# Layer slots reordered around one first-layer product: softmax moved, a PSUM bank changed, unread products added

## The chip, the cores and the metric

The kernel runs on one core of one Trainium2 chip, as one launch. The metric is the device time of that launch in microseconds. The core has a matmul engine (PE, with its weight loads PEld), a vector engine (DVE), a scalar engine (ACT), GpSimd (POOL) and a queue engine (SP) that issues DMAs; each works through its own queue in order.

## The reference

Three stages in a row, all float32:

```python
# 1 attention in chunks: 8 batches, 8 heads, 576 tokens in 9 chunks of 64, head size 64
scores = q_c @ k_c.T / 8
attn = exp(scores - max); attn /= sum + 1e-9
x = attn @ v_c                       # then laid out as 4608 tokens x 512
# 2 first layer, 512 -> 1024 -> 512
h = x @ w_in
solu = h * softmax(h)
ln = (solu - mean) / sqrt(var + 1e-6) * g_ln
y = ln @ w_out
# 3 second layer, 512 -> 1536 -> 512
out = (silu(y @ w_gate) * (y @ w_val)) @ w_out2
```

The weights come as float64 and are converted in the kernel.

## The kernel before

The 4608 tokens are 36 tiles of 128; three tiles make a group of 384 tokens (12 groups). Phase one (ph1) does attention and the first layer tile by tile and writes y to DRAM; phase two does the second layer for pairs of groups (lines 714 to 903) and is not touched by the change. Products that need float32 accuracy are split into a high and a low part in a reduced float32 format and done in three passes (`PASSES`, line 148).

The order on every engine is written out by hand: from `tc.manual_schedule()` (line 505) on, an instruction stands in its engine's queue where the program issues it. A buffer of a pool is handed to the next tile of the same tag when all readers of the old tile are done; an engine whose next instruction needs such a buffer stops until then, with all that is behind it.

What one tile t goes through:

- `load_qk`, `load_v`: 256 KB each on SP's queue.
- `scores(t)`: 32 small matmuls into one half of the PSUM tile `so_ps` (s_ps). `softmax(t)`: maximum and difference on DVE, exponential on ACT. `softmax_b(t)`: sum and reciprocal on DVE, the multiplication on POOL (line 299).
- `p_transpose(t)`: four PE transposes into the PSUM tile `pt` (line 307), then ACT copies it to `p` (line 309). `pv(t)`: 32 small matmuls of p and v into the other half of `so_ps` (o_ps). `x_split(t)`: ACT writes the high part of x, DVE (`x_low`) the low part.
- `hidden(t)`: the first layer's product of this tile, 24 matmuls of 512 columns (two halves of 12) into the PSUM tile `h`, of which there is one (two banks).
- `ln_max` (DVE), `ln_exp` (ACT), `ln_b` (DVE; its product with h, line 368, is the last reader of `h`), `ln_c` (a square on ACT, then seven instructions on POOL that end in line 392).
- `ln_T(t)`: eight PE transposes of the normalised tile into the PSUM tiles t0 and t1, the high part by ACT (line 411); the function that it returns, `ln_low`, makes the low part on DVE (line 416).
- `y_run`: the w_out products of a whole group, 24 matmuls of 384 columns for each 128 columns of y, in a PSUM pool of two banks with tag y (`ps_y`); at each 24th an ACT copy to SBUF (line 169) and a DMA to DRAM. `y_upto(t)` says how many are issued up to slot t: none before slot 4, 24 in each of slots 4 and 5, 48 in slot 6, then 32 a slot; the last 96, of group 11, belong to phase two's start (lines 892 to 894).

A slot works on several tiles at once. In the plain slot (lines 601 to 657, t from 4 on) PE's order is: scores(t+2), hidden(t), ln_T(t-1), pv(t+1), w_out products, and at the end p_transpose(t+2). In the same slots a weight of w_out or of the second layer is loaded (`w_raw`, two slots ahead), converted (`conv_start` a slot ahead on ACT and POOL, `conv_b` on DVE, `conv_c` on POOL) and split or spilled to DRAM (`todo2`, one slot later). PSUM is full: `so_ps` two banks, `h` two, t0, t1, and two for tag y. `pt` shares the tag y with the w_out products:

```python
pt = ps_y.tile([P, H, CH], F32, tag="y", name="pt")      # line 305
tr = ps_t.tile([P, 4, P], F32, tag=f"t{half}", name="tr") # line 405
ys[u] = ps.tile([P, TOK], F32, tag=ptags[...], name="y") # line 162
```

Slots 0 to 3 are `first_slot` (lines 659 to 692): no w_out products; softmax(t+1) is done at the head of slot t, behind it hidden(t), p_transpose(t+1), ln_T(t-1), pv(t+1) and scores(t+2). Slot 4 (`Y_AT`) is a plain slot with softmax(5), hidden(4) and p_transpose(5) put at its head (lines 607 to 611), so that it does two softmaxes. The prologue (lines 506 to 582) converts w_in into `wA` piece by piece, and does tile 0's and 1's attention and hidden(0) in its gaps. The end of phase one (lines 707 to 712) is the rest of `todo2`, then the last 32 w_out products but for group 11, then ln_T(35); phase two begins with SP's loads of y (`y_load`), the 96 products of group 11 and the preparation of y's operands (`y_prep`, lines 766 to 771).

Of the kernel before, what the change touches and what calls it, by code (L numbers as in the profile page):

```python
# [8 lines left out]
F32 = mybir.dt.float32  # L9
# [8 lines left out]
P = 128  # L18
CH = 64
GT = 3  # L20
W_OUT = 6
Y_AT = 4
# [4 lines left out]
def attn_moe_moe2_kernel(  # L27
# [16 lines left out]
    H = 8  # L44
# [193 lines left out]
    with ExitStack() as ph1:  # L238
# [63 lines left out]

        def p_transpose(t):
            e = st.pop(t).rearrange("p (n c) j -> p n (c j)", c=2)
            pt = ps_y.tile([P, H, CH], F32, tag="y", name="pt")
            for n in range(NP):
                nc.tensor.transpose(pt[:, 2 * n:2 * n + 2].rearrange("p h i -> p (h i)"), e[:, n], ident)  # L307
            p = att.tile([P, H, CH], F32, tag="p", name="p")
            nc.scalar.activation(out=p, in_=pt, func=AF.Copy)
            st["p", t] = p  # L310

        def pv(t):
            vv, p = vt.pop(t), st.pop(("p", t))
            for i in quads:
                quad(o_ps, vv, p, *i)

        def x_split(t):
            o = o_ps.rearrange("p c n i -> p n c i")
# [175 lines left out]
        def high(*ks):  # L494
            for k in ks:
                nc.scalar.activation(out=wA[:, k, 0, :], in_=cc[k], func=AF.Copy)
# [61 lines left out]
        clp(POOL, 6)  # L558
        add(5)
        hidden(0, (0,))  # L560
        softmax_b(1)
        shf(6)
        rnd(6)
# [12 lines left out]
        add(7)  # L576
        pv(1)
        x_low = x_split(1)
        high(7)
        rest(DVE, 7)  # L580
        hidden(0, (1,))
# [19 lines left out]
        def slot(t, todo2):  # L601


            todo, ahead = w_todo(t), t + 2 < NT
            cs = conv.pop(t)
            outs = [w2_out(u) if k == "2" else None for k, u in todo]
            if t == Y_AT:
                softmax(t + 1)
                softmax_b(t + 1)
                hidden(t)  # L610
                p_transpose(t + 1)
            if ahead:
                scores(t + 2)
                if t + 4 < NT:
                    load_qk(t + 4)
                softmax(t + 2)
            cs[:1] = [conv_c(c, o) for c, o in zip(conv_b(cs[:1]), outs)]
            if ahead:
                softmax_b(t + 2)
            for k, steps in todo2:  # L620
                if k == "o":
                    steps[1]()
            todo2 = [x for x in todo2 if x[0] != "o"]
            if t > Y_AT:
                hidden(t)
            ln_max(t)
            ln_exp(t)
            for k, steps in todo2:
                steps[0]()
            ln_low = ln_T(t - 1) if t >= 1 else None  # L630
            ln_b(t)
            x_low = None
            if t + 1 < NT:
                pv(t + 1)
                if t + 3 < NT:
                    load_v(t + 3)
                x_low = x_split(t + 1)
            if ln_low:
                ln_low()
            if x_low:  # L640
                x_low()
            ln_c(t)
            y0, y1 = y_upto(t - 1), y_upto(t)
            y2 = min(y1, -(-y0 // NY) * NY)
            y_run(wB, y0, y2, ps_y, att)
            for k, steps in todo2:
                steps[1]()
            if t + 1 < NT:
                conv_start(t + 1)
            cs[1:] = [conv_c(c, o) for c, o in zip(conv_b(cs[1:]), outs[1:])]  # L650
            y_run(wB, y2, y1, ps_y, att)
            for k, steps in todo2:
                steps[2]()
            if t + 2 < NT:
                raws[t + 2] = w_raw(t + 2)
                p_transpose(t + 2)
            return w_rest(todo, cs)

        def first_slot(t, todo2):


            todo = w_todo(t)
            cs = conv.pop(t)
            if t > 0:
                softmax(t + 1)
                for k, steps in todo2:
                    steps[1]()
                softmax_b(t + 1)
                conv_start(t + 1)
                hidden(t)  # L670
                p_transpose(t + 1)
            ln_max(t)
            ln_exp(t)
            cs = [conv_c(c) for c in conv_b(cs)]
            ln_low = ln_T(t - 1) if t > 0 else None
            x_low = None
            if t > 0:
                pv(t + 1)
            scores(t + 2)
            load_qk(t + 4)  # L680
            load_v(t + 3)
            if t > 0:
                x_low = x_split(t + 1)
            ln_b(t)
            if t > 0:
                x_low()
                ln_low()
            ln_c(t)
            if t == 0:
                conv_start(t + 1)  # L690
            raws[t + 2] = w_raw(t + 2)
            return w_rest(todo, cs)

        def w_rest(todo, cs):
# [8 lines left out]

        todo2 = []
        for t in range(NT):
            todo2 = (first_slot if t < Y_AT else slot)(t, todo2)
        for i in range(3):
            for k, steps in todo2:
                steps[i]()
        n = y_upto(NT - 1)  # L710
        y_run(wB, n, (NG - 1) * KD * NY, ps_y, att)
        ln_T(NT - 1)()

    with ExitStack() as ph2:
        cp = ph2.enter_context(tc.tile_pool(name="cp", bufs=2, reuse_waits="tile"))
# [231 lines left out]
```

## Time and profile before

| | us |
|---|---|
| runs (3): median, lowest, highest | 1413.26, 1412.28, 1418.31 |
| profiled execution: its own time, its span | 1411.09, 1409.3 |
| PE busy | 1344.0 (95% of the span), 9072 instructions |
| DVE, ACT, POOL busy | 847.8, 565.3, 468.4 |
| mean granted PE clock | 0.988 of full |
| PE busy in 0 to 40, 40 to 80, 80 to 117.5 | 16.87, 26.98, 29.18 |
| PE busy in 235 to 560 (325 us) | 314.54 |

The profile is of one execution. Phase one ends near 581 us. PE is the engine with the highest share; the first 117 us are the stretch in which it is often idle. A line of the order of time gives start, duration, engine, line, operation, output and inputs, the count of merged instructions, and in brackets how long the engine was idle before and what released it; a line with a count is merged, and its times are those of the whole stretch. The granted clock of PE is given as a share of its full rate.

### The profile page before, as it was taken

The numbers are of one execution on the slowest core, as the hardware profiler recorded it, in microseconds if no ns is written. First come the engines' busy times: TensorE is split into PE (matmuls) and PEld (weight loads), VectorE is DVE, ScalarE is ACT, GpSimd is POOL, SyncE is SP. The second block draws the span as 40 slices with busy tenths as digits, with TensorE's granted clock in tenths as the row PEclk, the third lists the DMA queues.
The fourth block names the chain that finished last, engine by engine and source line by source line (L and its number), as shares of the span: only waits on it lengthen the run. The fifth ranks groups of instructions, "written<-read, shape, count | busy, mean of one in ns | idle before, by whom it ended". The sixth has DMA issues, their size and how long they took to land.

```text
span 1409.3 us, 23612 instructions
## 1 busy us (share of the span) xinstructions
PE 1344.0 (95%) x9072; PEld 1226.5 (87%) x9072; DVE 847.8 (60%) x1540; ACT 565.3 (40%) x1144; POOL 468.4 (33%) x590
## 2 busy tenths in 40 slices
PE   3769999999999998999999999999999999999998
PEld 2558888888888888999999999998999899989997
DVE  6777776777777765544555465446444745464452
ACT  5554554545555554432332333223232332333221
POOL 5444354544545444321322241124121412232120
PEclk8899999999999999999999999999999999999999
DMA  6332446354556535966645554564547355635531
GB/s 231 105 134 93 161 152 220 128 194 161 193 184 198 180 122 175 396 241 243 213 149 183 207 178 158 200 212 148 194 164 246 118 196 188 223 134 185 197 105 45
DMA packets 91328, 252.15 MB, mean 179 GB/s; under 512 B 8272, under 2 KB 42064, under 8 KB 82000
## 3 DMA queue, kind: packets, MB, share of 16 engines
q1 hardware_dynamic: 84304, 241.21, 49.2%
q10 hardware_dynamic: 6912, 9.44, 1.9%
q8 instruction: 72, 1.18, 0.3%
q14 instruction: 40, 0.33, 0.1%
HBM read 203.43 MB, written 47.19 MB: 178 GB/s over the span
## 4 chain that ended last, share of the span: by engine, by line
PE 70%; DVE 2%; ACT 1%; POOL 1%; issue 1%; DMA 0%; ACTq 0%; SPq 0%; DVEq 0%; POOLq 0%
PE o L845 14%; PE pa L779 11%; PE pc L779 11%; PE pd L779 11%; PE tail L845 7%; PE pb L779 5%; PE y L163 5%; PE h L339 5%; PE so_ps L261 1%; PE tr L408 1%; DVE so L368 1%; DVE nm L350 1%; PE pt L307 0%; DVE blk L218 0%; ACT eh L357 0%
## 5 line engine op out<-in xcount | busy, mean ns | idle before, releaser
L339 PE MATMUL h<-wA,x 128*128 128x512 f32 x864 | 215.3, 406 | 12.4 <-DVE so L368 8.7
L163 PE MATMUL y<-lnT,wB 128*128 128x384 f32 x1152 | 210.7, 340 | 3.7 <-DVE lnT L416 3.7
L836 POOL TENSOR_TENSOR uflow<-sa,uflow 128x384 fp32r<-128x384 f32 x72 | 73.5, 1020 | 414.6 <-ACT uflow L807 393.5
L339 PEld LDWEIGHTS h<-wA,x 128*128 128x128 f32 x864 | 164.4, 194 | 50.4 <-ACT x L321 7.3
L163 PEld LDWEIGHTS y<-lnT,wB 128*128 128x128 f32 x1152 | 200.2, 189 | 6.0 <-DVE lnT L416 3.9
L779 PE MATMUL pa<-yk,wsa 128*128 128x384 f32 x864 | 175.1, 337 | 0.8 <-DVE osb L862 0.8
L779 PE MATMUL pd<-yk,wsb 128*128 128x384 f32 x864 | 173.0, 334 | 0.0
L836 DVE TENSOR_TENSOR uflow<-sb,uflow 128x128 fp32r<-128x128 f32 x72 | 28.2, 391 | 228.7 <-ACT uflow L834 228.7
L779 PEld LDWEIGHTS pa<-yk,wsa 128*128 128x128 f32 x864 | 153.3, 188 | 7.6 <-DVE osb L862 2.9
L779 PEld LDWEIGHTS pd<-yk,wsb 128*128 128x128 f32 x864 | 151.8, 188 | 0.0
L815 POOL TENSOR_TENSOR u<-u,p 128x384 f32<-128x384 f32 x72 | 72.9, 1013 | 192.6 <-DVE u L814 185.5
L804 ACT ACTIVATE p<-pa 128x384 f32<-128x384 f32 x72 | 35.4, 492 | 232.6 <-PE pa L779 231.0
L845 PE MATMUL o<-wo,uflow 128*128 128x512 f32 x504 | 122.8, 393 | 0.0
L845 PEld LDWEIGHTS o<-wo,uflow 128*128 128x128 f32 x504 | 94.1, 188 | 18.0
L357 ACT ACTIVATE eh<-h,nm 128x1024 f32<-128x1024 f32 x36 | 40.2, 1116 | 143.9 <-DVE nm L350 143.9
L817 ACT ACTIVATE sa<-pa 128x384 f32<-128x384 f32 x72 | 35.4, 492 | 150.1 <-PE pa L779 150.1
L845 PE MATMUL o<-uflow 128*128 128x512 f32 x360 | 87.5, 392 | 0.0
L779 PE MATMUL pb<-yk,wsa 128*128 128x384 f32 x432 | 86.5, 335 | 0.0
L779 PE MATMUL pc<-yk,wsa 128*128 128x384 f32 x432 | 86.5, 334 | 0.0
L779 PE MATMUL pc<-yk,wsb 128*128 128x384 f32 x432 | 86.5, 334 | 0.0
L818 DVE TENSOR_TENSOR sa<-pa,sa 128x384 f32<-128x384 f32 x72 | 40.2, 558 | 71.9 <-ACT sa L817 71.9
L845 PEld LDWEIGHTS o<-uflow 128*128 128x128 f32 x360 | 67.3, 188 | 13.1
(106 smaller groups left out, 2284.3 us busy)
## 6 DMA issues: line engine op xcount, KB each, us to landing
wsa<-ws SPq DMA_DIRECT2D x72, 1024.0 KB, 5.0
wsb<-ws SPq DMA_DIRECT2D x72, 768.0 KB, 6.0
ws<-shi SPq DMA_DIRECT2D x12, 896.0 KB, 4.4
raw<-in_moe_w_out SPq DMA_DIRECT2D x20, 512.0 KB, 6.9
qt<-in_q SPq DMA_DIRECT2D x36, 256.0 KB, 3.7
kt<-in_k SPq DMA_DIRECT2D x36, 256.0 KB, 4.1
vt<-in_v SPq DMA_DIRECT2D x36, 256.0 KB, 3.3
y<-ysb ACTq DMA_DIRECT2D x48, 192.0 KB, 2.7
```

The costliest lines, as they stand in the source:

```text
L163: nc.tensor.matmul(ys[u], lhsT=wB[:, f, a, d * P:(d + 1) * P], rhs=lnT[m][:, b, f, :], start=(n == 0), stop=(n == NY - 1),)
L261: nc.tensor.matmul(out[b * CH:(b + 1) * CH, c, n], lhsT=lhsT[r, h], rhs=rhs[r, h], start=True, stop=True, tile_position=(c * CH, b * CH),)
L339: nc.tensor.matmul(h[:, n * DM:(n + 1) * DM], lhsT=x[:, a, k, :], rhs=wA[:, n * KD + k, b, :], start=(i == 0), stop=(i == 3 * KD - 1),)
L350: nc.vector.tensor_reduce(out=nm, in_=h, axis=AX.X, op=ALU.max, negate=True)
L357: nc.scalar.activation(out=e, in_=h, func=AF.Exp, bias=nm, accum_out=se)
L779: nc.tensor.matmul(ps, lhsT=w[:, a, kk * P:(kk + 1) * P], rhs=yk[:, i, b, kk], start=(first and n == 0), stop=(n == 5), skip_group_check=True,
L804: nc.scalar.activation(out=p1, in_=psA, func=AF.Copy)
L815: nc.gpsimd.tensor_tensor(out=u3, in0=u3, in1=p5, op=ALU.add)
L817: nc.scalar.activation(out=sa, in_=psA, func=AF.Sigmoid)
L818: nc.vector.tensor_tensor(out=sa, in0=psA, in1=sa, op=ALU.mult)
L836: sub = lambda eng, o, x, h: eng.tensor_tensor(out=o, in0=x, in1=h.bitcast(F32), op=ALU.subtract)
L845: nc.tensor.matmul(o, lhsT=u[:, a, i * P:(i + 1) * P], rhs=wout(f)[:, b], start=(j0 and j == 0), stop=(j1 and j == 2),)
```

## The change

Six edits, all in phase one:

1. `pt` moves from the pool of tag y to the bank t1, which it shares in turn with the second half of `ln_T`.
2. `keep_warm(n)`: n matmuls of 512 columns on a fixed piece of `wA`, into a tile of tag y that nothing reads. 6 and 4 of them in the prologue, 12 in slot 0, 4 in each of slots 1 to 3, behind the scores.
3. `first_slot`: softmax(t+2) comes at the end of slot t, where before softmax(t+1) stood at the head of slot t. On DVE its maximum and difference are ahead of `ln_low`, its sum behind it.
4. Slot 4 is a function of its own, `turn_slot`: hidden(4) first; split of the w_out unit behind the exponential; softmax(6) ahead of ln_T(3), pv(5), ln_b(4); the weights' conversion behind; the w_out products ahead of conv_start(5); p_transpose(6) last.
5. The plain slot loses its special case for slot 4.
6. The end of phase one: half of the last 32 w_out products, ln_T(35), the other half, `ln_low`, and only then the rest of `todo2`.

```diff
--- before.py
+++ after.py
@@ -302,7 +302,7 @@
 
         def p_transpose(t):
             e = st.pop(t).rearrange("p (n c) j -> p n (c j)", c=2)
-            pt = ps_y.tile([P, H, CH], F32, tag="y", name="pt")
+            pt = ps_t.tile([P, H, CH], F32, tag="t1", name="pt")
             for n in range(NP):
                 nc.tensor.transpose(pt[:, 2 * n:2 * n + 2].rearrange("p h i -> p (h i)"), e[:, n], ident)
             p = att.tile([P, H, CH], F32, tag="p", name="p")
@@ -313,6 +313,14 @@
             vv, p = vt.pop(t), st.pop(("p", t))
             for i in quads:
                 quad(o_ps, vv, p, *i)
+
+        def keep_warm(n):
+
+            o = ps_y.tile([P, DM], F32, tag="y", name="warm")
+            for i in range(n):
+                nc.tensor.matmul(
+                    o, lhsT=wA[:, 0, 0, 0:P], rhs=wA[:, 0, 0, :], start=True, stop=True
+                )
 
         def x_split(t):
             o = o_ps.rearrange("p c n i -> p n c i")
@@ -558,6 +566,7 @@
         clp(POOL, 6)
         add(5)
         hidden(0, (0,))
+        keep_warm(6)
         softmax_b(1)
         shf(6)
         rnd(6)
@@ -576,6 +585,7 @@
         add(7)
         pv(1)
         x_low = x_split(1)
+        keep_warm(4)
         high(7)
         rest(DVE, 7)
         hidden(0, (1,))
@@ -604,11 +614,6 @@
             todo, ahead = w_todo(t), t + 2 < NT
             cs = conv.pop(t)
             outs = [w2_out(u) if k == "2" else None for k, u in todo]
-            if t == Y_AT:
-                softmax(t + 1)
-                softmax_b(t + 1)
-                hidden(t)
-                p_transpose(t + 1)
             if ahead:
                 scores(t + 2)
                 if t + 4 < NT:
@@ -621,8 +626,7 @@
                 if k == "o":
                     steps[1]()
             todo2 = [x for x in todo2 if x[0] != "o"]
-            if t > Y_AT:
-                hidden(t)
+            hidden(t)
             ln_max(t)
             ln_exp(t)
             for k, steps in todo2:
@@ -662,33 +666,63 @@
             todo = w_todo(t)
             cs = conv.pop(t)
             if t > 0:
-                softmax(t + 1)
                 for k, steps in todo2:
                     steps[1]()
-                softmax_b(t + 1)
                 conv_start(t + 1)
                 hidden(t)
                 p_transpose(t + 1)
             ln_max(t)
             ln_exp(t)
             cs = [conv_c(c) for c in conv_b(cs)]
-            ln_low = ln_T(t - 1) if t > 0 else None
-            x_low = None
             if t > 0:
+                ln_low = ln_T(t - 1)
                 pv(t + 1)
             scores(t + 2)
             load_qk(t + 4)
             load_v(t + 3)
             if t > 0:
                 x_low = x_split(t + 1)
+            keep_warm(4 if t else 12)
             ln_b(t)
             if t > 0:
                 x_low()
+            ln_c(t)
+            softmax(t + 2)
+            if t > 0:
                 ln_low()
+            else:
+                conv_start(t + 1)
+            softmax_b(t + 2)
+            raws[t + 2] = w_raw(t + 2)
+            return w_rest(todo, cs)
+
+        def turn_slot(t, todo2):
+
+            todo = w_todo(t)
+            cs = conv.pop(t)
+            hidden(t)
+            p_transpose(t + 1)
+            ln_max(t)
+            ln_exp(t)
+            for k, steps in todo2:
+                steps[1]()
+            scores(t + 2)
+            load_qk(t + 4)
+            load_v(t + 3)
+            softmax(t + 2)
+            ln_low = ln_T(t - 1)
+            pv(t + 1)
+            x_low = x_split(t + 1)
+            ln_b(t)
+            x_low()
+            softmax_b(t + 2)
+            ln_low()
             ln_c(t)
-            if t == 0:
-                conv_start(t + 1)
+            cs = [conv_c(c) for c in conv_b(cs)]
+            y_run(wB, 0, y_upto(t), ps_y, att)
+            conv_start(t + 1)
             raws[t + 2] = w_raw(t + 2)
+            p_transpose(t + 2)
             return w_rest(todo, cs)
 
         def w_rest(todo, cs):
@@ -703,13 +737,15 @@
 
         todo2 = []
         for t in range(NT):
-            todo2 = (first_slot if t < Y_AT else slot)(t, todo2)
+            todo2 = (first_slot if t < Y_AT else turn_slot if t == Y_AT else slot)(t, todo2)
+        n, end = y_upto(NT - 1), (NG - 1) * KD * NY
+        y_run(wB, n, (n + end) // 2, ps_y, att)
+        ln_low = ln_T(NT - 1)
+        y_run(wB, (n + end) // 2, end, ps_y, att)
+        ln_low()
         for i in range(3):
             for k, steps in todo2:
                 steps[i]()
-        n = y_upto(NT - 1)
-        y_run(wB, n, (NG - 1) * KD * NY, ps_y, att)
-        ln_T(NT - 1)()
 
     with ExitStack() as ph2:
         cp = ph2.enter_context(tc.tile_pool(name="cp", bufs=2, reuse_waits="tile"))
```

## Rows read from the trace of the kernel before

**Rows 1.** Waits of PE: engine, line, for whom: us in total, times, longest.

```profile
PE h L339 <- DVE so L368: 8.7, 4, 3.3
```

**Rows 2.** Windows: us, busy PE, PEld, DVE, ACT, POOL (instructions), PE clock, DMA share, GB/s.

```profile
27.00:47.40 20.40, 13.85 (x91) 9.72 (x92) 13.98 (x22) 10.75 (x20) 10.53 (x14) 0.50 0.19 65
47.40:98.60 51.20, 36.05 (x419) 29.79 (x417) 37.40 (x72) 25.67 (x48) 22.17 (x36) 1.00 0.37 124
98.60:105.50 6.90, 5.23 (x42) 4.25 (x43) 5.32 (x9) 5.68 (x11) 5.05 (x10) 0.51 0.28 105
...
235.20:238.60 3.40, 3.40 (x40) 2.66 (x39) 1.48 (x3) 0.60 (x2) 1.68 (x2) 0.50 1.04 343
...
562.80:566.30 3.50, 3.50 (x12) 3.50 (x12) 0.30 (x1) 0.00 (x0) 0.00 (x0) 0.51 1.00 278
566.30:1409.00 842.70, 838.30 (x4405) 783.22 (x4404) 438.16 (x822) 264.59 (x611) 204.40 (x192) 1.00 0.53 188
```

**Rows 3.** Groups of PE by form, 110 to 600 us: busy, mean ns | idle before.

```profile
L307 PE MATMUL pt<-ident,e 128*128 128x128 f32 x116 | 17.9, 278 | 12.4 <-ACT ysb L169 7.9 <-POOL rs L391 3.8 <-POOL t L388 0.4
```

**Rows 4.** Order of time, end of a plain slot near 280 us.

```profile
275.90 1.28 DVE L416 TENSOR_TENSOR lnT<-tr,lnT 128x512 fp32r<-128x512 f32 x2
...
280.54 0.47 ACT L169 ACTIVATE ysb<-y 128x384 f32<-128x384 f32 x1
...
281.15 0.63 PE L307 MATMUL pt<-ident,e 128*128 128x128 f32 x4 [2.41 <-ACT ysb L169]
...
281.82 0.60 ACT L309 ACTIVATE p<-pt 128x512 f32<-128x512 f32 x1 [0.81 <-PE pt L307]
```

**Rows 5.** Order of time, slots 0 to 2.

```profile
38.62 1.23 DVE L350 TENSOR_REDUCE nm<-h 128x1 f32<-128x1024 f32 x1 [1.99 <-PE h L339]
...
42.95 7.83 PE L339 MATMUL h<-wA,x 128*128 128x512 f32 x24 [3.30 <-DVE so L368]
...
49.36 1.04 POOL L299 TENSOR_TENSOR e<-e,r 128x512 f32<-128x512 f32 x1 [0.73 <-DVE r L298]
...
55.20 5.70 PE L339 MATMUL h<-wA,x 128*128 128x512 f32 x24 [2.02 <-DVE so L368]
...
62.88 0.66 PE L307 MATMUL pt<-ident,e 128*128 128x128 f32 x4 [1.97 <-POOL e L299]
...
63.57 0.60 ACT L309 ACTIVATE p<-pt 128x512 f32<-128x512 f32 x1 [2.48 <-PE pt L307]
...
64.06 1.11 ACT L357 ACTIVATE eh<-h,nm 128x1024 f32<-128x1024 f32 x1
...
67.12 5.72 PE L339 MATMUL h<-wA,x 128*128 128x512 f32 x24 [1.62 <-DVE so L368]
```

**Rows 6.** Order of time, slots 2 and 3: from the q load to product 4.

```profile
65.56 0.33 SPq L268 DMA_DIRECT2D qt<-in_q  x1
...
74.23 0.68 ACT L81 ACTIVATE m<-raw 128x512 f32<-128x512 f32 x1 [2.48 <-DMA raw<-in_moe_w_out]
...
77.74 1.09 ACT L357 ACTIVATE eh<-h,nm 128x1024 f32<-128x1024 f32 x1
...
80.78 5.73 PE L339 MATMUL h<-wA,x 128*128 128x512 f32 x24 [1.73 <-DVE so L368]
```

**Rows 7.** Order of time, slot 4 and the head of slot 5.

```profile
89.15 0.69 DVE L285 TENSOR_TENSOR e<-so_ps,mx 128x512 f32<-128x512 f32 x1
...
89.94 0.69 PE L261 MATMUL so_ps<-p,vt 64*64 64x64 f32 x32 [0.63 <-issue]
...
100.27 1.13 PE L261 MATMUL so_ps<-kt,qt 64*64 64x64 f32 x32 [4.83 <-DVE x L323]
101.33 7.65 PE L339 MATMUL h<-wA,x 128*128 128x512 f32 x24
```

**Rows 8.** Order of time, the seam of the phases.

```profile
555.05 1.20 POOL L392 TENSOR_SCALAR so<-so,nmu,rs 128x1024 f32<-128x1024 f32 x1
...
562.56 18.47 PE L163 MATMUL y<-lnT,wB 128*128 128x384 f32 x96 [3.70 <-DVE lnT L416]
...
577.46 0.55 DVE L769 TENSOR_TENSOR yk<-rawy,yk 128x384 fp32r<-128x384 f32 x1
```

## The prediction

> **What bounds the kernel now.** I read the waits of the matmul engine first: in its first 117 us it stands still again and again, and the row that names the tightest loop is the first layer's product waiting for the vector engine to finish with the one PSUM tile that holds it, 8.7 us in 4 times [rows 1]. Then the table of windows, for the clock. It shows 0.50 to 0.51 of full in four stretches, 20.4, 6.9, 3.4 and 3.5 us long, and from 566.3 us on 838.3 busy of 842.7 us at full clock [rows 2]: the second half has nothing to win and no edit touches it. Between 110 and 600 us the costliest idle group is the four probability transposes, 12.4 us ahead of them [rows 3], so a slot there is bound by the matmul engine and what it waits for. Last I read the order of time, to see what ends each wait. The whole effect must come from three places: the transposes' bank (slots 5 on), the start (to slot 6), and the seam to phase two.
>
> The sum is made against the profiled execution's own 1411.09 us (span 1409.3, 1.8 around it); the median shown, 1413.26, is 2.2 above it.
>
> **The transposes' bank.** At 278.7 the slot's last w_out product is done. Its eviction starts only at 280.54, behind other copies in ScalarE's queue, and the transposes start at 281.15, 0.14 after its end: idle 2.41 [rows 4]. They took turns with the w_out products in two banks. In their new bank they follow the second half of the LayerNorm transposes; its last reader is the vector engine's low part, over at 275.90 + 1.28 = 277.18 [rows 4], before the products end. So the wait goes, and nothing is late in its place: the scores behind the transposes wait for the low part of x, which comes after that same read in the vector queue, so even a late slot pays nothing more. The other direction: the LayerNorm transposes' second half now waits until ScalarE has copied p. That copy follows the eviction in the queue, and a whole product (5.7 us [rows 5]) lies between the two. Ends: back 12.4 in full, or nothing if the new wait is as long; I take -12.4. One of these gaps also let the clock fall: 235.2 to 238.6 ran at 0.50 [rows 2], 1.7 us lost, and with no gap there is no reason to fall. **-14.1, bounds 0 and -14.1.**
>
> **The start.** A full-clock product of 24 takes 5.70; the one at 42.95 took 7.83, 4.45 of it at half clock and 3.4 after [rows 2, 5]. That is 0.24 us for one matmul at full clock and 0.45 at half. The 26 unread products would cost 6.2 to 11.7 us if nothing covered them. They stand where the engine waits anyway: twelve (2.9 at full) in the 3.30 ahead of 42.95, four (1.0) in each of the 2.02, 1.62 and 1.73 ahead of 55.20, 67.12 and 80.78 [rows 5, 6], ten in the prologue's waits. I cost them at nothing at full clock; at half, four take 1.8 and are just too long.
>
> Slot 0 to 2: product 0's last six matmuls take 1.4 warm in place of 2.7, but wait for the last weights' preparation in between; of the 1.3 I keep 0.9. So product 1 starts 0.9 earlier (from a product's end to the next start stays 42.95 - 38.62 = 4.33) and takes 5.70 in place of 7.83: -3.0 at its end. Then GpSimd is late: the normalised e for tile 2 came at 49.36 + 1.04 = 50.40, 7.45 after the product's start [rows 5]. It stands behind the LayerNorm chain and a clamp that don't move; its softmax starts where it did, and only the split is taken out ahead of it, so 6.75 after. That is 1.05 after the product's end, and gives back 1 us. **H(2), start of product 2: -2.2.**
>
> Slots 2, 3: with the softmax made in the slot before, e is ready when the product ends. One turn is then 5.70 + 0.15 + 0.66 (transposes) + 0.60 (copy p, which is ahead of the exponential in ScalarE's queue) + 0.1 + 3.06 (exponential at 64.06 to the next product at 67.12) = 10.3, against 11.92 [rows 5]. But slot 3 has another bound that stays. Its conversion waits for the w_out load: first raw of two converted at 74.23, 8.67 after the q load was issued at 65.56, and the copy p and the exponential (77.74) queue behind it; product 4 follows 3.04 later, at 80.78 [rows 6]. The loads are issued when the scores of slot 2 are done, which comes 1.4 earlier in the slot. So over both slots only 1.4 of the gain is kept: H(4) -3.6. And the stops in slot 3 merge: transposes done at H(3) + 7, p there at H(3) + 11, a stop of 4 us where the old ones were at most 1.9. The clock held through stops of up to 2 us from 47.4 to 98.6 and fell in one of 4.83 [rows 2, 5, 7]. I expect a fall, which makes pv, scores and four unread products ahead of H(4) 1.6 longer: **H(4) -2.0.**
>
> Slot 4 (the turn): softmax 5 is gone from its head, split and softmax 6 come between exponential and the rest. In my count from H(4): product 5.70, p 7.1, exponential 8.2, split (two ScalarE and two vector ops, 1.5) 9.8, maximum and difference of softmax 6 11.25. PV of tile 5 must wait for that difference: before, it started at 89.94, right after the difference that ended at 89.15 + 0.69 [rows 7], although their halves of the tile differ. So 3.2 us of idle, then 24 w_out products (4.4), low parts of x and lnT until 16.7, transposes 6, scores 7: H(5) = H(4) + 18.0, against 20.55 [rows 6, 7]. The 3.2 us can drop the clock too; three times in four I charge 1.6: +1.2. Product 5 ran mostly at half clock before (7.65 [rows 7]) and now at full, but behind it the vector engine's maximum waits for the two units' clamps and adds on GpSimd, which come 9.5 after H(5) as now (9.3): of the 2 us about 1 is kept. On SP the loads of this slot are issued after the scores as before; the raw loads for slot 6 a few us later, none needed for 10 us. **Start of product 6: -4.0; bounds +1** (the clock falls in each of slots 1 to 4) **and -7** (in none).
>
> A rule against this part: the Trainium skill, TensorE: Matmul & The Clock Gate, part 4, says that a transpose doesn't count as matmul work for the clock. By it every burst of 12 transposes belongs to the stop beside it, and the clock falls in slots 1 and 2 as well. The trace disagrees so far: it stayed at 1.00 through just such bursts from 47.4 to 98.6 [rows 2].
>
> **The seam.** Before: 32 last products, the eight LayerNorm transposes, then a 3.70 wait for the vector engine's low part, and the half-clock stretch 562.8 to 566.3 right after [rows 2, 8], 1.7 lost. After: 16 products, the transposes, 16 products (2.8 at 0.174 each, the 96 of [rows 8] less that loss), and copy and low part (1.1 and 1.3) lie beside those. The transposes come 2.8 sooner, though, and need the last normalisation, over at 555.05 + 1.20 = 556.25; the products reach them at 555.15. So 1.2 of idle comes back: -2.4, and -1.7 for the clock. Moved behind the last product and the low part are the last unit's high and low copies and their two spill DMAs; SP issues phase two's loads of y after these, 0.5 later on the old scale, while the matmul engine is 4.1 ahead. The second half of the first y operand was ready at 577.46 + 0.55 [rows 8], for a product that started at 580.88: 2.9 of slack, so about 1.1 of waiting returns. **-3.0, bounds -1 and -4.1.**
>
> **Sum:** 14.1 + 4.0 + 3.0 = 21.1; 1411.1 - 21.1 = 1390.0, and 2.2 for the median: **1392**. Bounds: all terms at their best -25.2, 1388; the bank back in full as a new wait 1406.
>
> **Rivals.**
> (1) The start gives nothing: the clock falls in each long stop of slots 1 to 4, as by the rule above, and unread products at half clock stand in the way. H(6) at 0: 1396, at +1: 1397. For it: the merged stop in slot 3. Against: the four unread products refill exactly those stops. 15%.
> (2) The wait only moves: the transposes wait for the low part's read in place of the eviction. 12.4 + 1.7 gone: -7, 1406. Against: the read ended 3.97 us before the transposes started [rows 4]. 7%.
> (3) Slower: the shared bank stops the LayerNorm transposes' second half in each of the 31 slots from 5 on, until the copy p is done; PE is strictly behind it with pv and w_out products. It decides from the point where p lands later than 6.2 us after the product's start; p was being copied at 281.82, about when the next product starts, and would have to be 5 us later. Each us of lateness costs 31; from 0.7 a slot the gain is gone, at 1 us: 1392 + 31 = 1423. 3%.
> (4) The unread products don't do what they are for: the clock falls at 27 and rises at 47 as before. Product 1 stays at 7.8, -2 of H(2) is lost, H(6) loses no more than that since slot 3's load is then less late: 1394. 10%.
>
> My forecast has the other 65%. A change within 0.5% (7.1 us) is no change that a measurement can tell. Rivals 1 and 4 are faster by more, 2 lies on the line, 3 is split: faster 0.92, same 0.06, slower 0.02. Range: the bounds of the likeliest 1388 to 1398, the edge of rival 2 half taken in, and some below for a second profiled gap chain that I may have missed: 1384 to 1402.
>
> **What would show it.** Right: no idle ahead of the probability transposes after slot 6, clock 1.00 from slot 6 to the end, product 6 near 113.5, first yk product near 560. The bank is refuted by idle ahead of the transposes released by the low part (L416) or ahead of the second LayerNorm half released by p; the start by half clock between 27 and 47; slot 3 by an exponential that doesn't follow the raw load; the turn slot by a pv that starts before the softmax's difference ends. A time over 1402 would mean a new wait in slots 5 to 34.

## The result, and the profile after

The changed kernel takes 1397.74 us (median of 4 runs, 1397.12 to 1398.25) against 1412.77 for the kernel before (4 runs, 1411.06 to 1418.31) beside it. The ratio is 0.9887, 95% interval 0.9859 to 0.9915. That is 15.0 us faster where 21.1 were forecast: inside the range, 5.7 us above the forecast time. The profiled execution has a span of 1395.5 us, 13.8 below that of before, at a mean granted clock of 0.993 of full.

First the groups of the matmul engine (PE) by form, 105 to 600 us, of the kernel after: busy us, mean ns, and idle time before them, with its releaser.

```profile
L307 PE MATMUL pt<-ident,e 128*128 128x128 f32 x116 | 17.8, 277 | 5.3 <-DVE lnT L424 5.3
```

The 12.4 us of [rows 3] are gone. What is left is a single stop of 5.3, in slot 5. Next the windows of the start of the kernel after (us, busy PE, PEld, DVE, ACT, POOL with instructions, PE clock, DMA share, GB/s).

```profile
27.00:47.40 20.40, 16.08 (x124) 11.34 (x122) 15.66 (x25) 11.37 (x20) 11.53 (x15) 1.00 0.19 65
47.40:70.00 22.60, 19.59 (x210) 14.94 (x210) 20.79 (x36) 13.25 (x25) 12.61 (x22) 1.00 0.42 138
70.00:76.00 6.00, 3.54 (x68) 2.98 (x71) 3.69 (x7) 4.78 (x9) 2.78 (x3) 0.77 0.04 11
76.00:98.00 22.00, 18.86 (x197) 15.74 (x191) 15.93 (x33) 12.04 (x22) 8.73 (x17) 0.98 0.42 129
98.00:120.00 22.00, 16.71 (x132) 14.01 (x131) 16.40 (x28) 10.16 (x20) 11.57 (x16) 0.84 0.35 117
```

The first of them ran at 0.50 before [rows 2] and has the full 2.4 GHz now. The clock falls in two places, slots 3 and 5, and the order of time of PE shows a stop at each (product n is the first layer's product of slot n, the lines with `h`; they start with product 1):

```profile
41.81 5.72 PE L347 MATMUL h<-wA,x 128*128 128x512 f32 x24 [0.75 <-DVE so L376]
...
63.61 5.68 PE L347 MATMUL h<-wA,x 128*128 128x512 f32 x24 [0.30 <-DVE so L376]
...
73.41 1.11 PE L416 MATMUL tr<-ident,so 128*128 128x128 f32 x4 [2.46 <-ACT p L309]
...
77.54 5.62 PE L347 MATMUL h<-wA,x 128*128 128x512 f32 x24
...
88.42 0.69 PE L261 MATMUL so_ps<-p,vt 64*64 64x64 f32 x32 [3.08 <-DVE se L371]
...
94.73 5.78 PE L347 MATMUL h<-wA,x 128*128 128x512 f32 x24
...
111.66 1.09 PE L307 MATMUL pt<-ident,e 128*128 128x128 f32 x4 [5.29 <-DVE lnT L424]
...
113.74 7.55 PE L347 MATMUL h<-wA,x 128*128 128x512 f32 x24
```

Then the seam, PE's order of time from the last LayerNorm transposes to the first product of phase two, which answers to the 562.56 line of [rows 8]:

```profile
537.66 1.09 PE L416 MATMUL tr<-ident,so 128*128 128x128 f32 x8 [0.29 <-POOL so L400]
538.51 19.67 PE L163 MATMUL y<-lnT,wB 128*128 128x384 f32 x112
564.30 2.68 PE L815 MATMUL pa<-yk,wsa 128*128 128x384 f32 x6 [6.12 <-DMA wsa<-ws]
```

The wait of 3.70 for the vector engine is gone as intended, and a wait of 6.12 for a weight load stands in its place (`wsa` is a weight of the second layer, `yk` the operand that is prepared from y, `o` the last product, "out product" below). The difference of the two traces can be read off at a few instants (us, starts in the profiles). First the lines of the kernel before:

```profile
117.48 5.76 PE L339 MATMUL h<-wA,x 128*128 128x512 f32 x24
...
540.34 5.65 PE L339 MATMUL h<-wA,x 128*128 128x512 f32 x24
...
580.88 1.20 PE L779 MATMUL pa<-yk,wsa 128*128 128x384 f32 x6
...
595.43 2.92 PE L845 MATMUL o<-wo,uflow 128*128 128x512 f32 x12
```

and two of the kernel after that are not shown above:

```profile
522.50 5.65 PE L347 MATMUL h<-wA,x 128*128 128x512 f32 x24
...
581.68 2.92 PE L881 MATMUL o<-wo,uflow 128*128 128x512 f32 x12
```

| | before | after | gained |
|---|---|---|---|
| product 6 | 117.48 | 113.74 | 3.74 |
| product of slot 35, the last | 540.34 | 522.50 | 17.84 |
| first yk product of phase two | 580.88 | 564.30 | 16.58 |
| first out product | 595.43 | 581.68 | 13.75 |
| span | 1409.3 | 1395.5 | 13.8 |

So slots 6 to 34 gave 14.10 (forecast 14.1), the start 3.74 (forecast 4.0), and the seam took 4.09 back (forecast: 3.0 gained). The miss, some 7 us on the scale of the profiles, is the seam, from the last slot's product to the first out product: 55.09 us before, 59.18 after.

Why does the load come late? This is SyncE's queue of the kernel before at the seam, transfers with their issue times:

```profile
555.51 0.53 SPq L223 DMA_DIRECT2D ws<-shi  x1
...
561.97 5.79 SPq L753 DMA_DIRECT2D rawy<-y  x8
...
568.48 0.33 SPq L746 DMA_DIRECT2D wsa<-ws  x1
```

and of the kernel after:

```profile
544.29 0.53 SPq L223 DMA_DIRECT2D ws<-shi  x1
...
549.30 5.46 SPq L789 DMA_DIRECT2D rawy<-y  x8
...
558.88 0.32 SPq L782 DMA_DIRECT2D wsa<-ws  x1
```

Subtract the 17.84 by which phase one is ahead. The first spill would stand at 537.7 and is at 544.3; the loads of y at 544.1 and are 5.2 later; the first weight load at 550.6 and is 8.2 later. The spills moved are not the two of the forecast: the last slot's list holds the end of two units, five transfers of 896, 256, 256, 640 and 256 KB in the order of issue. The chain that ended last in the kernel after (start, us, what) says how one becomes the other (`blk` and `shi` are a weight on its way to a spill, `ysb` the copy of y that is stored):

```profile
543.00 1.27 ACT shi L222
...
544.29 1.49 DVE blk L227
...
546.73 5.30 DMA ws<-blk
...
552.13 0.50 ACT ysb L169
...
552.65 6.21 DMA y<-ysb
...
558.88 0.32 SPq L782
...
560.24 9.90 DMA wsa<-ws
```

A copy of y for the last group waits until a spill of 5.30 is over, its store takes 6.21, and only then does the first weight load go, at 558.88. The product that waited for it starts at 564.30, 5.4 later; the 9.90 at the end of the chain are the second such load, which holds up what comes behind. In this stretch the transfers have little room:

```profile
543.00:564.00 21.00, 15.18 (x88) 14.86 (x86) 8.14 (x9) 6.01 (x12) 7.23 (x7) 0.94 0.89 300
```

(a window of the kernel after: DMA share 0.89, 300 GB/s).

### The profile page after: what moved, and what is told of

Same layout as the page of the kernel before. It is cut to its first block, busy times and chain, and to the rows that moved or that the text cites. A ratio compares the mean times of both kernels' runs of the same rounds, so it can differ in the third digit from the quotient of the medians.

```text
span 1395.5 us, 23641 instructions
## 1 busy us (share of the span) xinstructions
PE 1348.6 (97%) x9106; PEld 1229.8 (88%) x9106; DVE 846.2 (61%) x1540; ACT 565.4 (41%) x1144; POOL 466.3 (33%) x590
## 4 chain that ended last, share of the span: by engine, by line
PE 89%; DMA 2%; DVE 1%; ACT 0%; POOL 0%; issue 0%; SPq 0%; ACTq 0%; DVEq 0%; POOLq 0%
PE o L881 14%; PE y L163 12%; PE h L347 12%; PE pa L815 11%; PE pc L815 11%; PE pd L815 11%; PE tail L881 7%; PE pb L815 5%; PE so_ps L261 3%; PE tr L416 2%; PE pt L307 1%; DMA wsa<-ws 1%; DMA y<-ysb 0%; DMA ws<-blk 0%; DVE osb L898 0%
## 5 line engine op out<-in xcount | busy, mean ns | idle before, releaser
L347 PE MATMUL h<-wA,x 128*128 128x512 f32 x864 | 211.4, 400 | 4.4 <-ACT x L329 1.4
```

Of the source, the lines that this page charges most:

```text
L347: nc.tensor.matmul(h[:, n * DM:(n + 1) * DM], lhsT=x[:, a, k, :], rhs=wA[:, n * KD + k, b, :], start=(i == 0), stop=(i == 3 * KD - 1),)
```

## The experiments

My theory (A): the new order of the seam costs these 7 us, because it puts five spills behind the last product and ahead of phase two's loads. The rival: arriving 18 us earlier, phase one meets transfers that don't come earlier, and any order would lose as much. A second question is which edits of the start give the 3.7 us. Ratios are to the kernel before, run beside them; spans and instants are of one profiled execution each; "seam" is the time from slot 35's product to the first out product.

| kernel | ratio, 95% interval | span | slot 35's product | seam |
|---|---|---|---|---|
| after | 0.9887, 0.9859 to 0.9915 | 1395.5 | 522.50 | 59.18 |
| after_again | 0.9907, 0.9886 to 0.9928 | 1395.3 | 520.93 | 60.57 |
| seam_old | 0.9887, 0.9870 to 0.9903 | 1393.2 | 522.92 | 56.45 |
| seam_spill | 0.9875, 0.9860 to 0.9889 | 1391.5 | 521.97 | 55.69 |
| bank | 0.9922, 0.9907 to 0.9937 | 1398.1 | 526.45 | 56.70 |
| nowarm | 0.9931, 0.9910 to 0.9953 | 1400.9 | 526.16 | 60.20 |
| oldorder_warm | 0.9897, 0.9876 to 0.9918 | 1395.7 | 525.17 | 56.70 |
| conv_late | 0.9894, 0.9870 to 0.9917 | 1396.9 | 522.46 | 60.65 |
| warm5 | 0.9898, 0.9862 to 0.9934 | 1396.6 | 522.24 | 59.68 |
| noturn | 0.9889, 0.9864 to 0.9914 | 1397.8 | 522.91 | 61.06 |
| early_spill | 0.9862, 0.9834 to 0.9890 | 1394.2 | 524.01 | 56.40 |
| early_warm5 | 0.9840, 0.9817 to 0.9863 | 1389.6 | 520.96 | 54.17 |
| seam_nospill | 0.9854, 0.9833 to 0.9875 | 1391.3 | 523.07 | 54.35 |

**The old seam under the rest of the change** (seam_old).

```diff
-        y_run(wB, n, (n + end) // 2, ps_y, att)
-        ln_low = ln_T(NT - 1)
-        y_run(wB, (n + end) // 2, end, ps_y, att)
-        ln_low()
...
+        y_run(wB, n, end, ps_y, att)
+        ln_T(NT - 1)()
```

> The changed kernel with the end of phase one as before (rest of todo2, then the 32 products, then ln_T(35)). Theory A, the new order of the seam itself costs: it puts the last unit's copies and five spill DMAs behind the last products, and phase two's loads behind those on SP. Then the old order follows the 17.8 us that phase one has gained: 1397.7 - 4.0 = 1393.7, first product of phase two at 563.0, no wait for wsa, wait of 3.7 for lnT back. Rival B, the loads of phase two can't come earlier whatever the order, because the DMA engines are full from there on: 1397.7 again, with the 6 us wait for wsa.

The seam is 56.45, 2.7 shorter than the changed one, and PE doesn't wait for the weights; its waits in this kernel, 530 to 580 us, are one row:

```profile
PE y L163 <- DVE lnT L424: 4.3, 1, 4.3
```

So most of the loss is the new order's. The old order itself takes 1.4 longer than before, but not for a load, as the rival would have it: the wait for the vector engine is 0.6 longer (4.32 for 3.70), and the 96 products behind it take 19.22 in place of 18.47, with the clock at 0.50 until about 550. The span is 2.3 below after's, the ratio is the same: the end times of these two alone don't part them.

**The spills first, then the new order** (seam_spill): the last unit's steps stand ahead of the first half of the products.

```diff
+        for i in range(3):
+            for k, steps in todo2:
+                steps[i]()
         y_run(wB, n, (n + end) // 2, ps_y, att)
         ln_low = ln_T(NT - 1)
         y_run(wB, (n + end) // 2, end, ps_y, att)
         ln_low()
-        for i in range(3):
-            for k, steps in todo2:
-                steps[i]()
```

> The changed kernel with the rest of todo2 ahead of the last products, then the new order (16 products, ln_T(35), 16 products, ln_low). Theory A: spills as early as before and the transposes covered: the forecast's -3.0 for the seam in place of +4.0, 1397.7 - 7 = 1390.7; first product of phase two near 561, wait there under 2 us. Rival B, loads bound by the DMA engines: 1397.7, wait for wsa 6 us.

The first spill is issued at 537.13, the weight load at 553.74, and the first yk product starts at 560.61, 3.7 before that of after. Its waits, 530 to 580 us:

```profile
PE pa L815 <- ACT p L840: 2.2, 1, 2.2
PE y L163 <- DVE lnT L424: 2.1, 1, 2.1
PE tr L416 <- POOL so L400: 1.1, 1, 1.1
```

The weight wait of 6.12 became three small ones, 5.4 together: with the steps put back in front, PE waits for LayerNorm's chain again (2.1 and 1.1), and a wait for phase two's own p appears.

**The same order without the spills' transfers** (seam_nospill), which tells the transfers (A1) from the copies and sums that were moved with them. This kernel leaves out the last five spills and fills their place in DRAM from the unit before, some slots earlier.

```diff
+        def dsts(j):
+            fs = () if f == FT - 1 else (f, f + 1) if f == FT - 2 else (f,)
+            return [wo_dram[i] if j == 2 else ws_dram[i].rearrange("p s b n -> p b s n") for i in fs]
...
-            nc.sync.dma_start(out=dst[:, 0], in_=hi.bitcast(F32))
+            for d in dsts(j):
+                nc.sync.dma_start(out=d[:, 0], in_=hi.bitcast(F32))
```

> The changed kernel in its own order, every copy of the seam in place, but without the last unit's five spill DMAs (that unit's place in DRAM is filled with the unit before it, some slots earlier, so the last weights of the second layer are those of the wrong unit). Theory A1, the spills' bytes and their place in SP's queue hold phase two's loads up: the loads of y are issued by 545 in place of 549 and the wait for wsa falls from 6 to 7.5 us to under 2; 1392 to 1393. Theory A2, the copies' new place in the queues of ScalarE and the vector engine does it: wait for wsa 4 us or more, 1396 to 1398.

The seam falls to 54.35. SyncE's queue of this kernel, with PE's first product of phase two:

```profile
543.75 4.67 SPq L795 DMA_DIRECT2D rawy<-y  x8
...
554.49 0.32 SPq L788 DMA_DIRECT2D wsa<-ws  x1
...
560.20 1.15 PE L821 MATMUL pa<-yk,wsa 128*128 128x384 f32 x4
```

and its waits, 505 to 582 us:

```profile
PE tr L422 <- POOL so L406: 1.7, 1, 1.7
PE pa L821 <- ACT p L846: 1.6, 1, 1.6
```

There is no wait for the weights, and the DMA share is 0.60 in 541 to 558 where after has 0.78 and after_again 0.87, while all copies and sums stay where after has them. So it is the transfers. Whether their bytes or the buffers that they hold cost more, this run doesn't part.

**The spills one slot earlier** (early_spill): the last units are spread over 29 slots in place of 30.

```diff
-            n = lambda t: max(0, min(3 * FT, (t - W2_AT + 1) * 3 * FT // (NT - W2_AT)))
+            n = lambda t: max(0, min(3 * FT, (t - W2_AT + 1) * 3 * FT // (NT - W2_AT - 1)))
```

> The changed kernel with the 36 second-layer weights spread over 29 slots in place of 30, so that nothing is left to copy and spill behind the last slot; the seam's new order stays. Theory A, the late spills put phase two's loads behind them in the DMA engines (from the first spill at 543 us to wsa's landing at 564 they are full): the wait for wsa (6 to 7.5 us) shrinks under 2 us, and the seam is worth the forecast's -3: 1397.9 - 6 = 1392. Rival B, the loads are bound by buffers that phase one still holds, or by their own bytes: wait for wsa stays at 5 us or more, 1397.

The seam is 56.40, the weight wait is gone, and the first spill is at 538.10. The cure adds no work, but it has a price: PE now waits 2.28 ahead of the last LayerNorm transposes for GpSimd's normalisation, which ends 17.1 after slot 35's product starts (15.1 in after). The first line is of this kernel; the second, of early_warm5 below, has the same wait, and only in the first do the transposes run slowly behind it (1.80 for 1.09; the clock of 541 to 558 is 0.90 here and 1.00 there):

```profile
541.16 1.80 PE L416 MATMUL tr<-ident,so 128*128 128x128 f32 x8 [2.28 <-POOL so L400]
538.11 1.09 PE L416 MATMUL tr<-ident,so 128*128 128x128 f32 x8 [2.28 <-POOL so L400]
```

The median is 1394.15 against 1398.03 of after_again; the two intervals overlap by 0.0004. This run reached slot 35 1.5 later than after (product 4 at 79.93 in place of 77.54), before anything that the edit touches.

**Which edits give the start its 4 us** (bank, nowarm, oldorder_warm). bank is the kernel before with the transposes' bank alone:

```diff
-            pt = ps_y.tile([P, H, CH], F32, tag="y", name="pt")
+            pt = ps_t.tile([P, H, CH], F32, tag="t1", name="pt")
```

> The kernel before with only the probability transposes' bank changed. By the forecast's term 14.1 less: 1412.8 - 14.1 = 1398.7, no idle ahead of these transposes after slot 6, clock 1.00 between 106 and 560. By the rival that the wait only moves (to the low part's read, or to the LayerNorm transposes' second half waiting for p): 1411 to 1413, idle of about 12 us under those names. If the bank also costs in slots 0 to 5, as the 5.3 us wait in slot 5 of the changed kernel may say, 1400 to 1402.

nowarm is the changed kernel without its unread products:

```diff
-        keep_warm(6)
...
-        keep_warm(4)
...
-            keep_warm(4 if t else 12)
```

> The changed kernel without any unread product. If they hold the clock up: it falls near 27 and is back near 44 to 47, product 1 starts at half clock, product 6 starts 2 to 4 us later, 1400 to 1401. If what follows (GpSimd in slot 1, the load in slot 3, the vector queue in slot 5) takes the difference up: product 6 within 0.5 us, 1397.5 to 1398.

oldorder_warm is the kernel before with the bank and these three lines, in the old order of softmax, slot 4 and seam:

```diff
+        keep_warm(6)
...
+        keep_warm(4)
...
+            keep_warm(4 if t else 12)
```

> The kernel before with the bank changed and the same unread products (6, 4, 12, 4, 4, 4), but the softmax where it was, slot 4 and the seam as before. If the unread products alone win the start: slot 35's product some 3.5 us ahead of the bank alone (526.5), 1396.5. If order and unread products only work together (the old order is bound by the late softmax, whatever the clock): within 1 us of the bank alone, 1399 to 1400.

Slot 35's product stands at 526.45 with the bank alone, 526.16 with the new order but no unread products, 525.17 with unread products but the old order, and at 520.9 to 523.1 in the five kernels that have both and are all but alike up to there. Together the two give 3.4 to 5.5. The new order alone shows nothing (0.3). The unread products alone give 1.3 in these traces, and the end times leave room for more: oldorder_warm has a median of 1396.73, bank 1400.23, with the same seam, and the intervals of their ratios overlap. nowarm itself scatters, from 1396.75 to 1403.26. So it is not shown that only the pair wins. Part of what nowarm lacks is the clock. A window of nowarm:

```profile
27.00:47.40 20.40, 13.91 (x94) 9.81 (x95) 14.91 (x25) 11.13 (x20) 10.53 (x14) 0.67 0.20 65
```

It is at 0.67 there, after at 1.00 (0.86 to 1.00 in the other kernels with both). In 70 to 98, nowarm and oldorder_warm are at 0.88 and after at 0.94, but this stretch explains nothing by itself: seam_old is at 0.82 there and has slot 35's product at 522.92. bank also confirms the largest term by itself: 540.34 - 526.45 = 13.9.

**The two stops that stay** (conv_late, warm5, noturn). conv_late issues the conversion of slots 1 to 3 behind the products, so that in slot 3 the copy p isn't queued behind it:

```diff
-                conv_start(t + 1)
...
-            else:
-                conv_start(t + 1)
+            conv_start(t + 1)
```

> The changed kernel with the next weight's conversion behind the normalisation in slots 1 to 3 too, as in slot 0, so that copy p and exponential no longer queue behind the load in slot 3. If that load is the bound of slot 3: product 4 starts 3 to 4 us earlier (73.5 to 74.5), no 2.5 us stop ahead of the LayerNorm transposes' second half, 1394.5 to 1395. If something else is late there (GpSimd, loads of q): product 4 within 1 us, 1397.

PE's order of time in it: the stop ahead of these transposes is 0.25 in place of 2.46.

```profile
72.81 0.66 PE L416 MATMUL tr<-ident,so 128*128 128x128 f32 x4 [0.25 <-ACT p L309]
```

The clock is 1.00 in 70 to 98 and product 4 starts 11.14 after product 3 (13.93 in after, 12.49 in after_again). Yet product 7 is at 132.27, where after has 132.31. Product 4 starts only 1.55 before that of after, since product 3 starts 1.24 later, and most of this is lost in slot 4, 18.41 long where after has 17.19, with a stop that after doesn't have there:

```profile
83.02 0.66 PE L307 MATMUL pt<-ident,e 128*128 128x128 f32 x4 [1.31 <-POOL e L299]
```

The conversion was the bound of slot 3, as expected; product 4 came 1.6 earlier, not 3 to 4. The median is 1395.58 against 1398.03 of after_again, with overlapping intervals: no gain is shown.

warm5 adds 20 unread products to the stop of slot 5:

```diff
+                if t == Y_AT + 1:
+                    keep_warm(20)
```

> The changed kernel with 20 unread products in slot 5, ahead of the probability transposes that stop 5.3 us there. If the stop's price beyond itself is the clock: 0.50 no longer seen from 112 to 117, slot 7's product 1.5 to 2 us earlier, 1396. If the products come too late or cost as much: 1397.7 or more.

```profile
109.54 4.74 PE L321 MATMUL warm<-wA 128*128 128x512 f32 x20
114.12 0.60 PE L307 MATMUL pt<-ident,e 128*128 128x128 f32 x4
...
115.27 5.76 PE L347 MATMUL h<-wA,x 128*128 128x512 f32 x24
```

They fill the stop, the clock holds at 1.00 in 98 to 120, product 6 takes 5.76 in place of 7.55, and slot 6 ends 1.5 to 1.8 sooner after its start (16.78 against 18.57 and 18.24). In the end time it doesn't show (1396.91, from 1393.40 to 1401.53): the clock was 0.79 in 76 to 98 in the profiled execution, and the seam waits 6.5 for its weights. noturn gives slot 4 the plain order:

```diff
+            if t == Y_AT:
+                hidden(t)
+                p_transpose(t + 1)
...
-            hidden(t)
+            if t > Y_AT:
+                hidden(t)
...
-            todo2 = (first_slot if t < Y_AT else turn_slot if t == Y_AT else slot)(t, todo2)
+            todo2 = (first_slot if t < Y_AT else slot)(t, todo2)
```

> The changed kernel with slot 4 as a plain slot (hidden(4) and the transposes of tile 5 ahead, the rest in the plain order), not turn_slot. If the turn slot's order wins time: product 7 some 2 to 4 us later than the changed kernel's 130.7 to 132.3, the end the same within 1 us since the seam holds phase two's start at 564: 1398. If it wins nothing: product 7 within 1 us.

Product 7 is at 132.72, among the 130.74 to 133.82 of the kernels with the turn slot and the unread products: reordering slot 4 wins nothing that can be told.

**The changed kernel again** (after_again), for the scatter.

> The changed kernel itself once more, beside the other runs of this call and against the kernel before on the same chip: ratio 0.989, product of slot 35 at 522.5, wait of about 6 us for wsa at the head of phase two.

It reached slot 35 1.6 sooner than the first time, and yet phase two began at 564.08 (564.30 the first time): it waited longer, for the same load.

```profile
PE pa L815 <- DMA wsa<-ws: 7.5, 1, 7.5
```

So in the changed kernel the transfers set when phase two begins, and what was won ahead of them here is lost there. Over all kernels the seam sorts by this: 59.18 to 61.06 in the six with the new order and late spills, 56.45 to 56.70 in the three with the old order, 54.17 to 56.40 in the four with the new order and the spills earlier or left out.

**Both cures** (early_warm5): the early spills and the 20 unread products together.

> early_spill with 20 unread products in slot 5 ahead of the probability transposes. With the seam no longer holding phase two's start, the 1.5 us that these won up to slot 7 now reach the end: 1.5 below early_spill, 1390.5. If the seam still holds it: same as early_spill.

0.984 (0.9817 to 0.9863) is the best of all, 1390.89 us. It beats the kernel before clearly; against the changed one it has the lower ratio in both of that kernel's timings, and its interval lies below the second's and overlaps the first's by 0.0004. Against early_spill beside it the median is 3.3 lower where 1.5 were expected; these intervals overlap, and the clock behind the stop of 2.28 differed too. Its waits at the seam, 505 to 582 us:

```profile
PE tr L416 <- POOL so L400: 2.3, 1, 2.3
PE pa L817 <- ACT p L842: 1.6, 1, 1.6
```

## Why the prediction was right and where it failed

The total lies inside the range, but not by the forecast's seam: the terms for slots 6 to 34 and for the start came out, and the seam went the other way. By its time alone 1397.74 is nearest to rival 1's 1396 to 1397; only the traces tell the two apart. Of the signs named, product 6 came at 113.74 (forecast 113.5), the first yk product at 564.30 (forecast 560).

**The bank: right, step and size.** There is no idle ahead of the transposes after slot 6, the clock is 1.00 from 120 to 558, and the gain is 14.10 in the trace and 13.9 alone for 14.1. The LayerNorm transposes never waited for the copy p in those slots; rivals 2 and 3 are out.

**The start: right in sum, by errors that cancel.** Products 1 and 2 came 1.14 and 2.36 earlier (forecast 0.9 and 2.2). Slot 3's merged stop and the loss of clock in it were as described, but smaller, 2.46 idle for 4: product 4 was 3.24 early in place of 2.0. In slot 4 the PV product did wait for the other half's difference, 3.08 for 3.2, and the clock held: product 5 at -6.6, forecast -4.55, or -3.35 with the 1.2 charged for the clock. That it held is luck in part: in five other kernels with this slot the same wait was 3.17, and the PV product behind it took 1.13 or 1.14 in place of 0.69. Slot 5 took 19.01, where -4.55 and -4.0 leave 16.7. (The forecast's own terms, -2.0, -2.55, +1.2 and -1, add up to -4.35, not -4.0.) The vector engine's maximum started 11.2 after product 5, forecast 9.5. The stop that stood at the end of slot 4 before (4.83 [rows 7]) now stands at the end of slot 5, 5.29 long, the clock falls in it, and product 6 takes 7.55 as product 5 took 7.65. That price was missing. It is not the bank's: in bank the stop of slot 4 only moves from the scores to the transposes, 4.80 for 4.83, as the sentence "even a late slot pays nothing more" has it:

```profile
100.14 1.08 PE L307 MATMUL pt<-ident,e 128*128 128x128 f32 x4 [4.80 <-DVE lnT L416]
```

**Rival 1 is out.** In the kernel after the clock is 1.00 from 27 to 70, through the stops of slots 1 and 2, and the start gave 3.74. The Trainium skill, TensorE: Matmul & The Clock Gate, part 4, says that transposes don't count as busy in the same way as matmuls. Read as the forecast read it, the bursts in slots 1 and 2 would have lengthened the stops beside them and the clock would have fallen there; the trace of after doesn't bear that out.

**Rival 4 is out, but its price was too low.** The unread products do hold the clock: 1.00 in 27 to 47, and 0.67 in nowarm. Without them slot 35 comes 3.1 to 5.2 later, where rival 4 put the loss at no more than 2. The order alone is not seen to win anything; how much of the gain needs both, the runs leave open.

**The seam: the failed step.** "Moved behind the last product and the low part are the last unit's high and low copies and their two spill DMAs; SP issues phase two's loads of y after these, 0.5 later on the old scale ... about 1.1 of waiting returns. -3.0". It measured +4.1. The count was wrong first: five transfers, 2304 KB. Then the place: the spills came 6.6 later and the loads of y 5.2, not 0.5, and I followed only the loads of y, not the weight load behind them, which came 8.2 later: it goes after a y store, and the copy for that store waits for a spill. The step's sum was off as well: 4.1 ahead and 0.5 late against 2.9 of slack is 1.7 of waiting, not 1.1. The idea of the step holds where the transfers are out of the way: seam_nospill has its first yk product 37.13 after slot 35's, before 40.54, 3.4 gained. But only 0.7 of that is left at the first out product (54.35 against 55.09), since from there to the first out product it takes 17.22 in place of 14.55, 1.64 of it a wait for p. And -3.0 was counted from a seam that doesn't stay as it was: arriving earlier, the old order takes 56.45 and 56.70. No run reached the forecast 52.1; the shortest seam is 54.17.

What stays open is why kernels that are all but alike up to slot 35 differ by up to 2 us there, and whether a fall of the clock in one stop rather than the next accounts for all of it.

## What to carry to other kernels

When a block of code is moved past a point where a phase ends, write out every transfer that it issues, in bytes, and follow each to the buffer that it frees and to whoever waits for that; the loads just behind it in the queue are not the only ones late. An operation that stands in the way of the matmul engine may still be cheaper to leave than to move behind it, or better to move a whole slot earlier, as the early spills did. And edits that work on the clock are to be tried together and apart: a stop refilled in one place may show nothing in the end time while another one still drops the clock, or while a wait behind it takes up the gain.

## What the runs showed of the hardware

The length of a stop alone didn't decide whether the clock fell. In 70 to 76 the kernel after had a stop of 2.46 and a clock of 0.77, after_again one of 2.24 and 1.00, conv_late 0.25 and 1.00; before, stops of up to 2.02 went with 1.00 [rows 2, 5]. The wait of 3.17 in slot 4 ended with a PV product of 0.69 in seam_nospill and of 1.13 in seam_old, and the wait of 2.28 at the seam with transposes of 1.80 in early_spill and of 1.09 in early_warm5.

Matmuls whose result nobody reads hold the clock like others: in warm5, 20 of them in 4.74 us, and 1.00 in 98 to 120 where the kernel after has 0.84; early_warm5 has 1.00 there too.

At 300 GB/s and a DMA share of 0.89 a transfer that takes its turn late wasn't late by its own length only: the spill of 5.30 and the store of 6.21 came one after the other ahead of the weight load, which PE then waited for until 564.30, and the next load took 9.90.
